# Pooled attention into a tanh-shrink MLP: group 0's second matmul, the x blocks of batch 1 and the loads around them in another order

## The chip, the cores and the metric

One NeuronCore of a Trainium2 chip. The metric is the device time of one launch in microseconds (us). The profile is one execution of the kernel, taken by the hardware profiler. Engines: PE (TensorE matmul; PEld is its weight load), DVE (VectorE), ACT (ScalarE), POOL (GpSimd) and SP (SyncE, which here only issues DMAs).

## The reference

`q`, `k`, `v` are (8, 8, 576, 64) float32: 8 batches, 8 heads, 576 rows, head width 64. `w_in` is 512 x 2048 and `w_out` 2048 x 512.

```
k_p = k.reshape(B, H, 72, 8, 64).mean(axis=3);  v_p likewise
scores = q @ k_p^T / 8;  attn = softmax(scores);  x = attn @ v_p
x = x.transpose(0, 2, 1, 3).reshape(4608, 512)
h = x @ w_in;  g = h - tanh(h);  out = g @ w_out       # out (4608, 512) float32
```

## The kernel before

**Work and tiling.** The 4608 rows are cut into nine groups of 512. Group g below 8 is the first 512 rows of batch g, and group 8 holds the last 64 rows of all eight batches. A group has two stages. The h stage computes 16 blocks of `h` (128 hidden columns by 512 rows, four matmuls each) with an ACT tanh and a DVE subtraction behind each, and leaves `Gt`. The output stage multiplies `Gt` by `w_out`. While group g is in its output stage, the attention of batch g+1 (scores, exp, product with v, normalising) is threaded between the matmuls, and the loads of batch g+2 run ahead of that.

**Order.** The schedule is written out by hand: each engine and each DMA queue executes its instructions in the order in which the Python code emits them, and semaphores are placed where one engine's data meets another's. So a move of a line in the code is a move in the in-order queue of every engine which that line uses.

**Group 0** is different from the others. Its output stage is direct: `mlp_o(0, tb, qd, gts)` (L611) is a unit of four 512-column matmuls, for row block `tb` (0 to 3) and a quarter `qd` of the hidden dimension. The quarters take `w2b` in the order of `W2_ORDER`, blocks 0, 8, 4, 12, which is the order in which the four parts of `w_out` arrive. Each row block has its PSUM bank (1, 2, 3, 0). With `qd == 3` the unit also copies the finished bank to `O`: on DVE for `tb` 0 and 1 (L626), on ACT for 2 and 3 (L628). The units double as filler between the steps of batch 1's attention (L1021 to L1085), which has to be done before group 1 can start:

- `k_transpose(1)`, `q_pe_transpose`, `q_pe_tail`, `scores_wide`, `scores_ends`: PE transposes and scores, evacuated by DVE and ACT.
- `pool_v1(0, 2)` and `pool_v1(2, 4)` (L300): DVE adds that pool `v_raw` and write `VB`, one half of the heads each. They wait for two POOL-queue loads of v.
- `av(1, blk, ...)` (L540): six matmuls `E` by `VB`, then on DVE a reciprocal (L522) and a multiplication (L523) into `x_sb`. `turn1(blk)` (L1000) transposes that block on PE (L566) and copies it on ACT into `xT[1]` (L573). Both take PSUM banks 4 to 7 in turn.
- `x_dma_transpose(1, 2)` and `k_dma_transpose(2)`: DMA transposes on SP's queue.
- `pool_k(2)`, `pool_v(2)`, `k_place(2)`: POOL work for batch 2, followed in group 1 by `v_spread(2)`, three small DMAs on POOL's queue that build `VB` for batch 2.

**Weight sums.** Groups 1 to 8 use a seven-product scheme for the output stage and need sums of quarters of `w_out`, kept in `w2s`. `sum0` to `sum3` (DVE, L673) build slots 0 to 3, in halves that start at hidden block 0 or 4; `negated` (ACT, L1004) builds slot 4; and `w_sum(b12, b22, b12, ALU.subtract)` replaces `b12` by `b22 - b12` in place, as one DVE instruction over all eight blocks. All must be emitted before group 1's products, and `b12` is also an input of `sum1`.

**Group 1's h stage** starts at L1087. `h_pair(1, p, b0, ...)` (L641) fills two PSUM banks, `b0` and `b0 + 1`, with b0 = 6, 4, 2, 6, 0, 2, 4 for p = 0 to 6; so p = 3 reuses the banks of p = 0, and p = 5 those of p = 2. ACT's tanh (L646) and DVE's subtraction (L647) read both banks; the bank pair is free when the subtraction is done. Between them ACT casts q of batch 2 for p = 2, 3, 4 (`q_cast_part`, L196 and L201) and SP issues its DMA transposes (L214, L219).

**Loads on SP's queue** around the change, in order: `load_k(2)` (held until the last v load of batch 1 has landed), `load_v(2)`, `load_q(2)`, the two transposes named above, `load_k(3)` (L1082), q's transposes of batch 2, both stores of group 0 (L1098, L1099), `load_v(3)`, `load_q(3)`. Later the transposes of batch 2's x (`x_dma_transpose`, L551) follow on the same queue, and group 2's first `h` matmuls wait for them.

**Start of the kernel.** The x of batch 0 is transposed on PE in four steps `x0_turn(blks, half, b0, eng)` (L939), through PSUM bank `b0` and an ACT copy into `xT[0]`; `h_part` (L958) computes the first blocks of `h` between them. `mlp_h(0, i, ...)` computes the later ones, in bank `i % 5`. `warm_pe` issues matmuls on zeros.

Of the kernel before, what the change touches and what calls it, by code (L numbers as in the profile page):

```python
# [12 lines left out]
ALU = mybir.AluOpType  # L13
# [14 lines left out]
TG = 512  # L28
# [15 lines left out]
def kernel(  # L44
# [9 lines left out]
    nc = tc.nc  # L54
# [9 lines left out]
    def bank(i, shape):  # L64
        n = 1
        for d in shape[1:]:
            n *= d
        v = PS[:, i, 0:n]
        if len(shape) == 3:
            return v.rearrange("p (a b) -> p a b", a=shape[1])  # L70
        if len(shape) == 4:
            return v.rearrange("p (a b c) -> p a b c", a=shape[1], b=shape[2])
        return v
# [226 lines left out]
    def pool_v1(ta, tb, eng=nc.vector):  # L300
        r = v_raw[1].rearrange("p t (j d) -> p t j d", d=D)
        for n in (4, 2, 1):
            eng.tensor_tensor(  # L303
                out=r[:, ta:tb, 0:n, :],
                in0=r[:, ta:tb, 0:n, :],
                in1=r[:, ta:tb, n : 2 * n, :],
                op=ALU.add,
            )
        if ta == NM:
            return v_left(VB[1], r[:, NM, 0:1, :], eng)  # L310
        return v_main(VB[1], r[:, ta:tb, 0:1, :], nc.vector, ta, tb)
# [228 lines left out]
    def av(b, blk, alloc, both):  # L540
        x_sb = x_block(b, blk)
        if both:
            av_both(b, blk, x_sb)
        else:
            for half in range(2):
                av_half(b, blk, half, x_sb, alloc)
        return x_sb
# [57 lines left out]
    def mlp_h(g, i, gts, pool):  # L605
        mlp_h_mms(g, i, 0, NFB, pool)
        mlp_h_act(i, gts)
# [3 lines left out]
    def mlp_o(g, tb, qd, gts):  # L611
        if qd == 0:
            o_tiles[tb] = bank((1, 2, 3, 0)[tb], [128, DM])
        o_ps = o_tiles[tb]
        i0 = W2_ORDER[qd]
        for i in range(i0, i0 + 4):
            nc.tensor.matmul(
                o_ps[:, :],
                lhsT=gts[i][:, tb * 128 : (tb + 1) * 128],
                rhs=w2b[:, i, :],  # L620
                start=(i == 0),
                stop=(i == NHID - 1),
            )
        if qd == 3:
            if tb < 2:
                nc.vector.tensor_copy(out=O[:, tb, :], in_=o_ps[:, :])  # L626
            else:
                nc.scalar.copy(out=O[:, tb, :], in_=o_ps[:, :])  # L628

    def h_mms(g, i, dst, t0=0, t1=4):  # L630
        x = xT[g % 2] if g < NB else xT_last
# [40 lines left out]
    def w_sum(out, a, b, op, eng=nc.vector, k0=0, k1=NP):  # L672
        return eng.tensor_tensor(  # L673
            out=out[:, k0:k1, :], in0=a[:, k0:k1, :], in1=b[:, k0:k1, :], op=op
        )
# [136 lines left out]
    for m, base, step, cm in (  # L812
# [6 lines left out]
            out=m,  # L819
            in_=m,  # L820
# [118 lines left out]
    def x0_turn(blks, half, b0, eng):  # L939
        n = len(blks)  # L940
        ps = bank(b0, [128, 2, n, 128])
        for i, blk in enumerate(blks):
            for f in range(2):
                nc.tensor.matmul(
                    ps[:, f, i, :],
                    lhsT=x0[:, blk, half, 2 * f : 2 * f + 2, :].rearrange("p h d -> p (h d)"),
                    rhs=ident[:, :],
                    start=True,
                    stop=True,
                )  # L950
        eng(
            out=xT[0][:, blks[0] : blks[0] + n, 2 * half : 2 * half + 2, :].rearrange(
                "p i f c -> p f i c"
            ),
            in_=ps,
        )
# [11 lines left out]
    x0_turn((0, 1), 0, 0, nc.scalar.copy)  # L968
    av_pair(1, 1, 1)
    warm_pe(1, b0=5)  # L970
    x0_turn((2, 3), 0, 0, nc.scalar.copy)
    for i, b0 in ((0, 6), (1, 7), (2, 5)):
        h_part(i, 0, 0, b0)
    x0_turn((0, 1), 1, 4, nc.scalar.copy)
    h_part(3, 0, 0, 3)
    for i in range(3):
        h_part(i, 0, 1)
    x0_turn((2, 3), 1, 0, nc.scalar.copy)
    nc.scalar.copy(out=q_bf[:QT, R, :, :], in_=t0[:QT, :, R, :])
    h_part(3, 0, 1)  # L980
    for i in range(4):
# [6 lines left out]
    mlp_h(0, 4, gts, bank(4, [128, TG]))  # L988

    for i in range(5, NHID):  # L990
        mlp_h(0, i, gts, bank(i % 5, [128, TG]))
        if i == 7:
            q_pe_tail(0)
        if i == 9:
            scores_tail(0)
        if i == 11:
            ps_a.n = 0
            av(0, 4, ps_any, True)
            x_dma_transpose(0, 2)
    def turn1(blk):  # L1000
        x_pe_transpose(1, blk, x_pairs[1, blk // 2][:, blk % 2])

    def negated(n):
        nc.scalar.mul(  # L1004
            out=w2s[:, 4, 4 * n : 4 * n + 4, :], in_=b22[:, 4 * n : 4 * n + 4, :], mul=-1.0
        )

    ps_a = Banks(4, 5, 6, 7)
    def sum0(k0):
        return w_sum(w2s[:, 0, :, :], b11, b22, ALU.add, k0=k0, k1=k0 + 4)  # L1010

    def sum1(k0):
        return w_sum(w2s[:, 1, :, :], b11, b12, ALU.add, k0=k0, k1=k0 + 4)

    def sum2(k0):
        return w_sum(w2s[:, 2, :, :], b21, b22, ALU.add, k0=k0, k1=k0 + 4)
# [13 lines left out]
    k_transpose(1, ps_any, (nc.vector.tensor_copy, nc.vector.tensor_copy))  # L1030
    q_pe_transpose(1, (0, 1), "act")
    mlp_o(0, 3, 0, gts)
    pool_v1(0, 2)
    q_pe_transpose(1, (2, 3), "act")
    q_pe_tail(1)
    scores_wide(1, (0,))
    sum1(0)
    mlp_o(0, 0, 1, gts)
    scores_wide(1, (1,))
    mlp_o(0, 1, 1, gts)  # L1040
    scores_wide(1, (2, 3))
    scores_ends(1)
    negated(0)
    sum2(0)
    sum0(0)
    sum3(0)
    pool_v1(2, 4)
    mlp_o(0, 2, 1, gts)
    mlp_o(0, 3, 1, gts)
    mlp_o(0, 0, 2, gts)  # L1050
    mlp_o(0, 1, 2, gts)
    ps_a.n = 0
    after(load_k(2), v1_last)
    load_v(2)
# [2 lines left out]
    av(1, 1, ps_any, True)  # L1057
    sum1(4)
    sum0(4)
    mlp_o(0, 2, 2, gts)  # L1060
    turn1(0)
    mlp_o(0, 3, 2, gts)
    turn1(1)
    av(1, 2, ps_any, True)
    av(1, 3, ps_any, True)
    negated(1)
    sum3(4)
    mlp_o(0, 0, 3, gts)
    turn1(2)
    mlp_o(0, 1, 3, gts)  # L1070
    turn1(3)
    av(1, 4, ps_any, True)
    x_pairs.pop((1, 0))
    x_pairs.pop((1, 1))
    x_dma_transpose(1, 2)
    pool_k(2, nc.gpsimd)
    k_dma_transpose(2)
    mlp_o(0, 2, 3, gts)
    mlp_o(0, 3, 3, gts)
    sum2(4)  # L1080
    w_sum(b12, b22, b12, ALU.subtract)
    load_k(3)  # L1082
    pool_v(2, nc.gpsimd, (0, 1))
    k_place(2, nc.gpsimd.tensor_copy)
    pool_v(2, nc.gpsimd, (2,))  # L1085
# [1 line left out]
    for g in range(1, NG):  # L1087
        nb = g + 1 if g + 1 < B else None
        nn = g + 2 if g + 2 < B else None
        for p in range(NP - 1):  # L1090
            if g == 1 and 2 <= p < 5:
                q_cast_part(2, p - 2)
                q_dma_transpose(2, p - 2)
            if nb is not None and g > 1 and p < 3:
                q_cast_part(nb, p)
            h_pair(g, p, ((6, 4, 2, 6, 0, 2, 4) if g == 1 else (0, 2, 4, 6, 0, 2, 4))[p], p % 2)
            if g == 1 and p == 4:
                store(0, 0, 2, nc.sync)  # L1098
                store(0, 2, 4, nc.sync)  # L1099
                load_v(3)  # L1100
                load_q(3)
                v_spread(2, nc.gpsimd)
            if 3 <= p < 6:
                sum_p(2 * p - 6, 2 * p - 4)
            if g > 1 and p == 0:
                if nb is not None:
                    k_dma_transpose(nb)
                store(g - 1, 2, 4, nc.gpsimd)
                store(g - 1, 0, 2, nc.gpsimd)
                if nb is not None:  # L1110
                    k_place(nb, nc.gpsimd.tensor_copy)
            if nb is not None and g > 1 and p < 3:
                q_dma_transpose(nb, p)
            if nb is not None and g > 1 and p == 2:
                v_spread(nb)
                if nn is not None:
                    load_k(nn)
                    load_v(nn)
                    load_q(nn)
        h_one(g, NP - 1, 1, 0, 2)  # L1120
        h_one(g, NP - 1, 0, 1, 3)
        sum_p(6, 8)
        sum_q(0, 4)
        sum_q(4, 8)
        if nb is not None:
            sum_d(0, 2)
            sum_d(2, 4)
        ps_a = Banks(2, 3, 4, 5, 0, 1)
        for u in range(14):
            n, half = u // 2, u % 2  # L1130
            bk, lhs, rhs = products[n]
            if n == 6 and g == NG - 1:
                break
            product(g, bk, lhs, rhs, 4 * half, 4 * half + 4, n < 2)
            if half:
                after_product(g, n)
            if nb is not None:
                if u == 0:
                    head_scores(nb, (0, 1))
                if u == 2:  # L1140
                    head_scores(nb, (2, 3), True)
                if u in (5, 6, 7, 8, 10):
                    blk = (5, 6, 7, 8, 10).index(u)
                    av(nb, blk, ps_b1, True)
                    if blk in (1, 3, 4):
                        x_dma_transpose(nb, blk // 2)
                if u == 6 and nn is not None:
                    pool_k(nn, nc.gpsimd)
                    pool_v(nn, nc.gpsimd)
        if g < NG - 1:  # L1150
            nc.scalar.copy(out=O[:, 0:2, 0:HD], in_=chain(g, C1))  # L1151
# [37 lines left out]
```

## Time and profile before

| what | value |
| --- | --- |
| median of 3 runs | 285.57 us (285.42 to 286.19) |
| the profiled execution | 285.73 us, span 283.9 us |
| granted TensorE clock | 1.00 |
| PE busy | 274.5 us, 97% of the span |
| DVE, ACT, POOL busy | 79%, 55%, 42% |
| HBM read, written | 36.70 MB, 9.44 MB |

The span runs from the first to the last instruction that the profile holds; 1.8 us of the profiled execution lie around it. A line of a timeline gives the start, the duration, engine, code line, operation, output and input tiles, shapes and a count; a bracket at its end is the idle time of the engine before it and what ended that. A duration counts waiting inside the engine too. Matmul durations include the pipeline's drain, so consecutive matmuls overlap: the distance between starts is their real cost.

Landmarks in the span: group 0's h stage ends and its output stage starts at 32.01 us; group 1's h stage starts at 52.96, its products at 67.52; group 2's h stage starts at 82.50. Each later group takes about 28.8 us up to the last ones.

### The profile page before, as it was taken

The page shows a single profiled execution, that of the slowest core. Times are in us where ns is not written, and L with a number is a line of the kernel's source. Part 1 is how long each engine was busy: PE and PEld are TensorE (multiplying, and loading weights), DVE is VectorE, ACT ScalarE, POOL GpSimd, SP SyncE. Part 2 cuts the span into 40 slices and gives each one's busy share as a digit, 9 for nine tenths or more (in the row PEclk, how much of TensorE's full clock was granted, in tenths as well). Part 3 has the DMA queues.
Part 4 walks back from the last instruction along what each step waited for, and adds up shares of the span by engine and source line. Part 5 has one row for each costly group of instructions (what it writes and reads, how often), then busy time and mean ns, then how long its engine had stood idle before and what let it go on. Part 6 is the DMA issues. An engine that isn't in the chain of part 4 may idle for free.

```text
span 283.9 us, 5492 instructions
## 1 busy us (share of the span) xinstructions
PE 274.5 (97%) x2174; PEld 180.9 (64%) x2174; DVE 224.2 (79%) x337; ACT 154.8 (55%) x207; POOL 118.5 (42%) x132
## 2 busy tenths in 40 slices
PE   7999998999999999999999999999999999999993
PEld 2574544645884589448944895489547954884583
DVE  5758968999966997599859985998599849936983
ACT  4757482487437662766285718670867056216610
POOL 8853601992497029801990199009900210010000
PEclk9999999999999999999999999999999999999999
DMA  6999999899968794789488948896640440011014
GB/s 247 236 212 277 225 243 279 240 216 270 275 98 198 245 311 89 172 257 328 85 134 300 333 85 136 250 331 133 125 151 1 77 157 2 0 72 79 0 39 111
DMA packets 66491, 49.82 MB, mean 175 GB/s; under 512 B 42104, under 2 KB 55944, under 8 KB 66466
## 3 DMA queue, kind: packets, MB, share of 16 engines
q1 hardware_dynamic: 55538, 33.87, 46.9%
q0 software_dynamic: 8736, 13.77, 19.8%
q10 hardware_dynamic: 2192, 1.84, 2.2%
q8 instruction: 17, 0.28, 0.4%
q14 instruction: 8, 0.07, 0.1%
HBM read 36.70 MB, written 9.44 MB: 163 GB/s over the span
## 4 chain that ended last, share of the span: by engine, by line
PE 75%; DMA 12%; DVE 9%; POOL 2%; issue 1%; SPq 0%; DVEq 0%
PE PS L633 37%; PE PS L690 33%; DMA v_raw<-in_v_dram 8%; PE PS L446 3%; PE PS L472 2%; DVE w2s L673 2%; DMA k_raw<-in_k_dram 2%; DMA xT<-x_sb 2%; DVE x_sb L523 2%; DVE v_raw L303 1%; DVE w2b L673 1%; DVE rden L522 0%; DVE O L626 0%; DVE Gt L647 0%; POOL w2s L841 0%
## 5 line engine op out<-in xcount | busy, mean ns | idle before, releaser
L633 PE MATMUL PS<-xT,w1b 128*128 128x512 bf16 (+1 forms) x504 | 98.3, 355 | 1.1 <-DVE Gt L647 0.6
L647 DVE TENSOR_TENSOR Gt<-PS,TS 128x1024 bf16<-128x1024 f32 x56 | 68.3, 1220 | 32.2 <-ACT TS L646 32.1
L633 PEld LDWEIGHTS <-w1b 128*128 128x128 f16 x576 | 56.3, 98 | 54.2 <-issue 1.5
L646 ACT ACTIVATE TS<-PS 128x1024 f32<-128x1024 f32 x56 | 57.4, 1024 | 30.8 <-PE PS L633 28.2
L734 POOL TENSOR_TENSOR m<-O,m 128x512 f32<-128x512 f32 x6 | 7.6, 1261 | 77.1 <-ACT m L732 63.7
L690 PE MATMUL PS<-w2s,Dg 128*128 128x256 f16 x256 | 30.2, 272 | 0.0
L467 ACT ACTIVATE E<-PS 72x1024 bf16<-72x1024 f32 (+1 forms) x30 | 26.1, 930 | 3.9 <-PE PS L446 3.7
L690 PEld LDWEIGHTS <-Gt 128*128 128x128 bf16 x256 | 23.5, 98 | 7.0 <-issue 2.5
L261 POOL TENSOR_TENSOR k_raw<-k_raw 128x512 f32<-128x512 f32 (+2 forms) x13 | 21.1, 1638 | 16.3 <-DMA k_raw<-in_k_dram 16.3
L690 PEld LDWEIGHTS <-P 128*128 128x128 bf16 x256 | 24.5, 98 | 3.0
L690 PEld LDWEIGHTS <-Dg 128*128 128x128 bf16 x256 | 24.6, 98 | 2.8
L655 DVE TENSOR_TENSOR P<-Gt 128x1024 bf16<-128x1024 bf16 x32 | 21.9, 686 | 0.5
L706 POOL DMA_DIRECT2D out_dram<-O x14 | 7.7, 554 | 31.6 <-DVE O L744 29.5
L741 ACT COPY m<-PS 128x512 f32<-128x512 f32 x8 | 4.7, 586 | 29.6 <-PE PS L690 29.6
L665 DVE TENSOR_TENSOR Dg<-Gt 128x1024 bf16<-128x1024 bf16 x32 | 20.4, 681 | 0.0
L523 DVE TENSOR_TENSOR x_sb<-PS,rden 128x512 bf16<-128x512 f32 x28 | 19.4, 691 | 1.0
L282 POOL TENSOR_TENSOR v_raw<-v_raw 128x512 f32<-128x512 f32 (+1 forms) x12 | 19.6, 1656 | 0.0
L690 PE MATMUL PS<-w2s,Gt 128*128 128x256 f16 x128 | 16.4, 273 | 0.0
L690 PE MATMUL PS<-w2b,P 128*128 128x256 f16 x128 | 16.3, 273 | 0.0
L690 PE MATMUL PS<-w2b,Gt 128*128 128x256 f16 x128 | 16.3, 272 | 0.0
L690 PE MATMUL PS<-w2s,Q 128*128 128x256 f16 x128 | 16.3, 272 | 0.0
L1151 ACT COPY O<-PS 128x512 f32<-128x512 f32 x7 | 4.1, 586 | 21.9 <-PE PS L690 21.9
(124 smaller groups left out, 400.4 us busy)
## 6 DMA issues: line engine op xcount, KB each, us to landing
k_raw<-in_k_dram SPq DMA_DIRECT2D x7, 1024.0 KB, 5.9
out_dram<-O POOLq DMA_DIRECT2D x14, 512.0 KB, 4.3
v_raw<-in_v_dram SPq DMA_DIRECT2D x6, 1024.0 KB, 8.1
q_raw<-in_q_dram SPq DMA_DIRECT2D x6, 1024.0 KB, 11.4
w1b<-in_moe_w_in_dram POOLq DMA_DIRECT2D x4, 512.0 KB, 13.3
w2b<-in_moe_w_out_dram POOLq DMA_DIRECT2D x4, 512.0 KB, 21.8
v_raw<-in_v_dram POOLq DMA_DIRECT2D x2, 512.0 KB, 21.2
out_dram<-O SPq DMA_DIRECT2D x2, 512.0 KB, 4.2
```

The lines of the kernel that those rows point to most:

```text
L261: eng.tensor_tensor(out=r[:, ta:tb, 0:4, :], in0=r[:, ta:tb, 0:4, :], in1=r[:, ta:tb, 4:8, :], op=ALU.add,)
L282: eng.tensor_tensor(out=r[:, ta:tb, 0:4, :], in0=r[:, ta:tb, 0:4, :], in1=r[:, ta:tb, 4:8, :], op=ALU.add,)
L446: nc.tensor.matmul(dst, lhsT=kv[a * D : (a + 1) * D, m, :], rhs=rhs, start=True, stop=True,)
L467: nc.scalar.activation(out=e, in_=ps, func=ACT.Exp, scale=SCALE)
L523: nc.vector.tensor_tensor(out=x_sb[:, :, :, :], in0=ps[:, :, :, 0:D], in1=rden[:, :, :, :].to_broadcast([128, 2, 4, D]), op=ALU.mult,)
L633: nc.tensor.matmul(dst[:, t0 * 128 : t1 * 128], lhsT=w1b[:, fb, i * 128 : (i + 1) * 128], rhs=x[:, t0:t1, fb, :], start=(fb == 0), stop=(f ...
L646: nc.scalar.activation(out=t2, in_=PS[:, b0 : b0 + 2, :], func=ACT.Tanh)
L647: nc.vector.tensor_sub(out=Gt[:, p, :, :], in0=PS[:, b0 : b0 + 2, :], in1=t2)
L655: nc.vector.tensor_tensor(out=P[:, a:b, :], in0=Gt[:, a:b, 0, :], in1=Gt[:, a:b, 1, :], op=ALU.add)
L665: return nc.vector.tensor_tensor(out=Dg[:, a:b, :, :], in0=Gt[:, a:b, :, 0:HT], in1=Gt[:, a:b, :, HT:TG], op=ALU.subtract,)
L673: return eng.tensor_tensor(out=out[:, k0:k1, :], in0=a[:, k0:k1, :], in1=b[:, k0:k1, :], op=op)
L690: nc.tensor.matmul(part(g, bk, tt), lhsT=lhs(k, slice(tt * 128, (tt + 1) * 128)), rhs=rhs[:, k, :], start=(first and k == 0 and (tt == 0 o ...
```

## The change

- `mlp_o` copies all four finished banks on ACT.
- In the start, two of the four `x0_turn` go through bank 5 instead of 0, the third block of `h` moves from bank 5 to 0, and block 5 of `h` from bank 0 to 5.
- `sum1(0)`, `sum2(0)`, `sum0(0)` are emitted ahead of `pool_v1(0, 2)`, instead of behind it; `sum3(0)` stays.
- The remaining units of group 0 come about one unit earlier against batch 1's steps: one more unit stands ahead of `av(1, 0)`, one now stands between `av(1, 2)` and `av(1, 3)`, and none of the last ones is left behind `k_dma_transpose(2)`. `negated(1)` moves ahead of `av(1, 2)`.
- The two stores of group 0 are issued on SP as soon as their units are emitted: the first ahead of `av(1, 3)`, the second behind `x_dma_transpose(1, 2)`; before, both stood in group 1 behind `h_pair` p = 4.
- `load_k(3)` moves from behind the weight sums into group 1 behind `h_pair` p = 4, directly ahead of `load_v(3)`; that is behind q's transposes of batch 2.
- The in-place `w_sum` is cut in two: blocks 0 to 3 where it was, blocks 4 to 7 behind `h_pair` p = 0 of group 1.

```diff
         if qd == 3:
-            if tb < 2:
-                nc.vector.tensor_copy(out=O[:, tb, :], in_=o_ps[:, :])
-            else:
-                nc.scalar.copy(out=O[:, tb, :], in_=o_ps[:, :])
+            nc.scalar.copy(out=O[:, tb, :], in_=o_ps[:, :])
...
     warm_pe(1, b0=5)
-    x0_turn((2, 3), 0, 0, nc.scalar.copy)
-    for i, b0 in ((0, 6), (1, 7), (2, 5)):
+    x0_turn((2, 3), 0, 5, nc.scalar.copy)
+    for i, b0 in ((0, 6), (1, 7), (2, 0)):
         h_part(i, 0, 0, b0)
...
-    x0_turn((2, 3), 1, 0, nc.scalar.copy)
+    x0_turn((2, 3), 1, 5, nc.scalar.copy)
...
-        mlp_h(0, i, gts, bank(i % 5, [128, TG]))
+        mlp_h(0, i, gts, bank(i % 5 if i > 5 else 5, [128, TG]))
...
     mlp_o(0, 3, 0, gts)
+    sum1(0)
+    sum2(0)
+    sum0(0)
     pool_v1(0, 2)
     q_pe_transpose(1, (2, 3), "act")
     q_pe_tail(1)
     scores_wide(1, (0,))
-    sum1(0)
     mlp_o(0, 0, 1, gts)
     scores_wide(1, (1,))
     mlp_o(0, 1, 1, gts)
     scores_wide(1, (2, 3))
     scores_ends(1)
     negated(0)
-    sum2(0)
-    sum0(0)
     sum3(0)
     pool_v1(2, 4)
     mlp_o(0, 2, 1, gts)
     mlp_o(0, 3, 1, gts)
     mlp_o(0, 0, 2, gts)
     mlp_o(0, 1, 2, gts)
+    mlp_o(0, 2, 2, gts)
     ps_a.n = 0
     after(load_k(2), v1_last)
     load_v(2)
...
     sum1(4)
     sum0(4)
-    mlp_o(0, 2, 2, gts)
+    mlp_o(0, 3, 2, gts)
     turn1(0)
-    mlp_o(0, 3, 2, gts)
+    mlp_o(0, 0, 3, gts)
     turn1(1)
+    negated(1)
     av(1, 2, ps_any, True)
+    mlp_o(0, 1, 3, gts)
+    store(0, 0, 2, nc.sync)
     av(1, 3, ps_any, True)
-    negated(1)
     sum3(4)
-    mlp_o(0, 0, 3, gts)
     turn1(2)
-    mlp_o(0, 1, 3, gts)
+    mlp_o(0, 2, 3, gts)
     turn1(3)
     av(1, 4, ps_any, True)
     x_pairs.pop((1, 0))
     x_pairs.pop((1, 1))
     x_dma_transpose(1, 2)
+    mlp_o(0, 3, 3, gts)
+    store(0, 2, 4, nc.sync)
     pool_k(2, nc.gpsimd)
     k_dma_transpose(2)
-    mlp_o(0, 2, 3, gts)
-    mlp_o(0, 3, 3, gts)
     sum2(4)
-    w_sum(b12, b22, b12, ALU.subtract)
-    load_k(3)
+    w_sum(b12, b22, b12, ALU.subtract, k1=4)
...
             h_pair(g, p, ((6, 4, 2, 6, 0, 2, 4) if g == 1 else (0, 2, 4, 6, 0, 2, 4))[p], p % 2)
+            if g == 1 and p == 0:
+                w_sum(b12, b22, b12, ALU.subtract, k0=4)
             if g == 1 and p == 4:
-                store(0, 0, 2, nc.sync)
-                store(0, 2, 4, nc.sync)
+                load_k(3)
                 load_v(3)
                 load_q(3)
                 v_spread(2, nc.gpsimd)
```

## The prediction, made before the run

> **What bounds the kernel now.** I read the page, then the list of waits of PE, then the timelines of all engines from 32 to 84 us, and the DMA issues. The page first:
>
> ```profile
> PE 274.5 (97%) x2174; PEld 180.9 (64%) x2174; DVE 224.2 (79%) x337; ACT 154.8 (55%) x207; POOL 118.5 (42%) x132
> ```
>
> PE has 9.4 us of idle time in 283.9. From group 2 on, the chain of waits runs through PE alone to the last copy, so whatever PE saves before 84 us should arrive at the end. The waits of PE:
>
> ```profile
> PE PS L487 <- DVE VB L323: 1.1, 1, 1.1
> PE PS L633 <- DVE Gt L647: 0.6, 1, 0.6
> PE PS L633 <- DMA xT<-x_sb: 0.5, 1, 0.5
> ...
> PE PS L487 <- ACT xT L573: 0.2, 1, 0.2
> ```
>
> All four lie between 43 and 84 us. The first three in PE's timeline, with the matmuls ahead of two of them:
>
> ```profile
> 43.51 0.34 PE L487 MATMUL PS<-VB,E 128*128 128x130 bf16 x3
> 44.95 0.68 PE L487 MATMUL PS<-VB,E 128*128 128x130 bf16 x9 [1.10 <-DVE VB L323]
> ...
> 58.89 8.79 PE L633 MATMUL PS<-xT,w1b 128*128 128x512 bf16 x40 [0.57 <-DVE Gt L647]
> ...
> 82.50 1.04 PE L633 MATMUL PS<-xT,w1b 128*128 128x256 bf16 x8
> 84.03 13.12 PE L633 MATMUL PS<-xT,w1b 128*128 128x256 bf16 x64 [0.49 <-DMA xT<-x_sb]
> ```
>
> Costs by distance of starts in that timeline: an mlp_o unit 0.87 (46.62 to 47.48), an av 0.35 (50.88 to 51.23), a turn 0.24 (46.38 to 46.62). So the waits really cost more than the brackets say: 44.95 - (43.51 + 3 x 0.058) = **1.27**; at 48.54 (waiting for ACT's copy of xT) 48.54 - (47.70 + 9 x 0.058) = **0.32**; at 58.89, where p 0 to 2 need 1.74 + 2 x 1.73, 58.89 - 58.16 = **0.73**; at 84.03, 84.03 - (82.50 + 8 x 0.1085) = **0.66**.
>
> Behind the second stands DVE, held up by POOL:
>
> ```profile
> 53.88 1.61 DVE L673 TENSOR_TENSOR w2s<-w2b 128x1024 f16<-128x1024 f16 x1
> 55.42 2.29 DVE L673 TENSOR_TENSOR w2b<-w2b 128x2048 f16<-128x2048 f16 x1
> 57.62 3.59 DVE L647 TENSOR_TENSOR Gt<-PS,TS 128x1024 bf16<-128x1024 f32 x3
> ...
> 51.45 1.88 POOL L267 TENSOR_TENSOR k_raw<-k_raw 128x640 f32<-128x640 f32 x1
> 53.41 1.53 POOL L270 TENSOR_TENSOR kd<-k_raw 128x640 bf16<-128x640 f32 x1
> 54.90 4.47 POOL L282 TENSOR_TENSOR v_raw<-v_raw 128x512 f32<-128x512 f32 x2
> ```
>
> The same sum of 1024 columns takes 0.6 while POOL is idle (four in 2.40 at 40.65 in the chain). Here it ends 0.55 after POOL's L270 (54.94, 55.49), the next POOL instruction ends 1.13 after that (56.62), the 2048-column sum 1.09 after that (57.71): the two engines take turns.
>
> **What the Trainium skill says.** "SBUF — State Buffer", section "Who interferes with whom": a DVE instruction with two SBUF inputs and a GpSimd instruction that reads SBUF exclude each other, each for its whole length. The trace agrees to the 0.01 us just given. "DMA: Bandwidth & Descriptors", section "Queues, rings and completion order": descriptors of one queue are consumed in ring order, and a DMA engine takes turns between queues. The trace agrees with the first: q of batch 3, issued at 68.49, lands after 10.8 us at 79.3, and both x transposes issued behind it (76.87, 79.13) take 4.9 us instead of 3.1 in the next group. Turn-taking between queues is not shown cleanly.
>
> **Part by part.**
>
> *Banks of x0_turn.* The second turn waits for ACT's copy out of bank 0 (15.89 + 0.59 = 16.48; it starts at 16.53), where PE would be free at 16.26: 0.2 us. But PE then waits at the k transposes for kd, which DVE ends at 34.50 behind a DMA (PE: 34.60), and at the first unit of quarter 1 (37.11) for w2b, issued at 12.99 and landing 24.1 later, 37.09. Worth **0.0**; were that load sooner, -0.2.
>
> *Three sums ahead of pool_v1(0, 2).* DVE idles 2.61 us (36.09 to 38.70) for v. sum1 fits at once, sum2 and sum0 need the weights of 37.09: done by 38.3, still ahead of v. Behind VB's first half (40.65) only sum3 remains, to 41.3, and the second half of v lands at 22.7 + 19.6 = 42.3. pool_v1(2, 4) takes 1.86 (43.05 to 44.91), so VB is ready at 44.2 instead of 44.9. One more unit in front puts av(1, 0) at 43.51 + 0.87 = 44.38, its second half at 44.55. **The 1.27 go**, with 0.3 to spare.
>
> *Units between the steps.* PE now runs av 0 and 1 to 45.08, a unit to 45.95, turn 0 at 45.97 (x_sb: second half 44.55 + 0.44 + 0.24 + 0.69 = 45.92), a unit, turn 1, av 2 to 47.66, a unit to 48.53, av 3 (ACT's turn 1 copy is done at 48.3: **the 0.32 go**), turn 2, a unit to 49.98, turn 3 at 50.11 (DVE's x_sb at 50.07, a new wait of 0.13), av 4, a unit: group 1 starts at **51.57 instead of 52.96**. ACT carries two more copies (2 x 0.59, from DVE's 2 x 0.67) and negated's 1.06 sooner; its queue (0.5 a copy) ends turn 3's copy at 51.2 and the last copy of O at 52.2, ahead of PE's need (51.57 for bank 6 and the first two blocks, 52.0 for bank 7) and of the first tanh (53.6). Nothing queued there delays PE.
>
> *DVE up to Gt of p 0.* sum3(4) still waits for POOL and ends at 51.92; POOL's k load (48.3) hasn't moved. The two O copies (1.27) are gone, so av 4's multiplication ends at 52.8, and sum2 takes its turn at POOL's next end: 53.33 to 53.88. L270 then to 55.28, the half w_sum to 55.83, Gt of p 0 to 56.98 (1.15 as before). PE wants p 3 at 51.57 + 5.20 = 56.77, and gets it at 57.02 instead of 58.89: **gain 1.87 up to here**, the wait being 0.25 now.
>
> *The second half of w_sum* then asks for the port at about 56.9; POOL's L282 ends 55.83 + 1.13 = 56.96. **The order is not shown by any row.** If DVE gets it, w_sum costs 0.55 and Gt of p 2 ends at about 59.9, ahead of PE's p 5 (57.02 + 3.46 = 60.48): nothing lost. If POOL gets it, w_sum waits for L282's second half (1.66): Gt p 1 60.4, Gt p 2 61.6, and p 5 waits 1.16. I take the first, since DVE's next instruction shows up 0.09 before its predecessor's end, POOL's only 0.04.
>
> *Stores.* Two of 0.5 MB, issued at 49.8 and 54.0 on SP instead of 65. In ring order they stand behind q of batch 2 (lands 44.84 + 11.4 = 56.2) and fill a gap: 84 to 116 GB/s from 54 to 58. Cost on q **0**; without ring order, up to 1.05 MB at 340 GB/s (319 to 353 in the stretches from 44 to 54), 3.1 us. On SP, the first store waits for ACT's second copy and nothing is ready behind it before x_end at 52.8; the second is reached at 54.0, after its copy (52.2) and before kd (55.3), so neither holds up a transpose's issue. They delay the k transpose behind them to about 61.5, which POOL wants at 60.8 (k_place), so v_spread moves 0.7 later.
>
> *load_k(3)* leaves the place ahead of q's transposes, which then land by about 65; needed at 66.6. It starts at 62 with v and q behind. Group 2's row of loads took 14.0 from the first issue (93.50) to q's landing (96.03 + 11.5 = 107.5), so q lands at 76 to 77 instead of 79.3. x's second transpose, issued 1.87 sooner at 77.26, lands at 80.4 to 81.7; PE needs it at 82.50 - 1.87 + 0.87 = 81.5. **0.5 of the 0.66 go.** POOL wants k at 74.5; it lands at about 68.
>
> *Sum* on the profiled execution: 285.73 - 1.87 - 0.5 = 283.4; this execution lies 0.16 over the median, so **283.2**.
>
> **Rivals.**
>
> 1. *POOL gets the port first*: 1.87 - 1.16 + 0.5 = 1.2 gained, **284.3**. For it: the two requests lie within 0.1 us.
> 2. *The stores share bandwidth with q of batch 2.* q 3.1 late gives tanh of p 2 at 61.3, Gt at 62.6, p 5 waits 2.1: 285.57 - 1.87 + 2.1 - 0.5, about **285.3**. Against it: the ring order seen with the x transposes.
> 3. *v_spread becomes the bound; slower.* Its three small DMAs go over POOL's queue, at 64 to 65.5. Before, only stores and the start of v's load were near, and the last landed after 2.6 us (67.4). Now 3.4 MB on SP's queue are under way until about 76.5. av of batch 2 needs VB at 74.21 - 1.87 = 72.3. If the small packets are held back until the loads drain, av waits 4.2: 285.57 - 1.87 + 4.2, **287.9** with the x wait kept. It decides the sign from a landing at about 74.2 on. Against it: turn-taking, as the skill states, would cost only some 3 us.
> 4. *The order changes but the landings rule*: v's second half or kd land as much later as PE comes sooner; **285.5**. Against it: those loads don't depend on PE.
>
> **Numbers.** Forecast 0.47 (own range 282.7 to 283.8), rival 1 0.27 (283.9 to 284.7), rival 2 0.10, rival 3 0.09, rival 4 0.07. A difference of 0.3%, 0.86 us, is about what a measurement of this kernel can tell from no change. Faster (below 284.7): 0.47 + 0.26 + 0.01 = 0.74; slower (above 286.4): 0.09 and 0.02 of rival 2's upper end, 0.11; the rest 0.15. Range 282.6 to 285.4: it leaves out rival 3, part of rivals 2 and 4, and the tail below.
>
> **What would show it.** The VB wait and the ACT xT wait gone from PE's waits, group 1's first h matmul at 51.6, p 3 at 57.0, two DVE w2b sums with the second at 57 (or at 58.7: rival 1, with a wait of PE at L633 near 60.5), q's casts no later than 56.3 (else rival 2), the xT wait at most 0.2. Wrong would be a wait of PE at L472 on VB (rival 3), or group 1 starting as late as before.

## The result, and the profile after

| kernel | median us (range, runs) | ratio to before (95% interval) |
| --- | --- | --- |
| before | 285.57 (285.02 to 286.19, 7) | |
| changed | 284.43 (283.54 to 284.93, 7) | 0.9957 (0.9938 to 0.9977) |

The change saves 0.43%, 1.14 us (the interval is 0.66 to 1.77 us), where 2.37 were forecast (285.57 - 283.2). Executions more than 1.5% slower than the fastest of the same kernel are left out of all medians and ratios, here and below. The profiled execution of the changed kernel took 284.74 us with a span of 282.9. In its code the lines behind `mlp_o` stand three lower: L633 is L630, L647 L644, L673 L670, L690 L687.

Its waits of PE, in the columns total, times, longest:

```profile
PE PS L352 <- DVE kd L270: 1.4, 1, 1.4
...
PE PS L630 <- DMA xT<-x_sb: 0.5, 1, 0.5
```

Three of the four waits of before are gone: L487 for VB, L487 for xT, L633 for Gt. The xT wait of 0.5 stayed. New at the top is L352, the transposes of k ahead of batch 1's scores, which wait for `kd`. PE's timeline from there to group 2:

```profile
31.48 2.75 PE L617 MATMUL PS<-w2b,Gt 128*128 128x512 f16 x12
35.65 0.45 PE L352 MATMUL PS<-ident,kd 128*128 128x128 bf16 x5 [1.41 <-DVE kd L270]
...
45.48 0.86 PE L487 MATMUL PS<-VB,E 128*128 128x130 bf16 x12
...
52.67 14.00 PE L630 MATMUL PS<-xT,w1b 128*128 128x256 bf16 x72
66.50 1.04 PE L687 MATMUL PS<-w2s,Gt 128*128 128x256 f16 x8
...
81.57 1.04 PE L630 MATMUL PS<-xT,w1b 128*128 128x256 bf16 x8
83.09 3.19 PE L630 MATMUL PS<-xT,w1b 128*128 128x256 bf16 x18 [0.48 <-DMA xT<-x_sb]
```

The line at 45.48 holds both halves of two av without a stop between them; before, the second half stood still for VB. The line at 52.67 is the h stage of group 1 without a stop, up to its products. The same points of both profiles, side by side:

| point of PE | before | changed | gain so far |
| --- | --- | --- | --- |
| group 0's output stage starts | 32.01 | 31.48 | 0.53 |
| transposes of k (L352) | 34.60 | 35.65 | -1.05 |
| group 1's h stage starts | 52.96 | 52.67 | 0.29 |
| its products start | 67.52 | 66.50 | 1.02 |
| group 2's h stage starts | 82.50 | 81.57 | 0.93 |
| the matmul behind the xT wait | 84.03 | 83.09 | 0.94 |
| end of the span | 283.9 | 282.9 | 1.0 |

From L352 to group 1 the changed kernel takes 17.02 instead of 18.36: **1.34 gained**, where the prediction had 52.96 - 51.57 = 1.39. From group 1's start to its products it takes 13.83 instead of 14.56: **0.73 gained**, the p 3 wait. But PE was already 1.05 behind the old kernel when that stretch began, since `kd` was late, and nothing came at xT.

DVE's timeline answers the question who gets the port that DVE and POOL share:

```profile
54.38 2.03 DVE L670 TENSOR_TENSOR w2b<-w2b 128x1024 f16<-128x1024 f16 x1
56.34 1.21 DVE L644 TENSOR_TENSOR Gt<-PS,TS 128x1024 bf16<-128x1024 f32 x1
57.47 0.68 DVE L670 TENSOR_TENSOR w2b<-w2b 128x1024 f16<-128x1024 f16 x1
```

The second half of `w_sum` took 0.68: DVE had the port at once, at 57.47. POOL's second L282 starts at 57.52 and has to wait for it, 2.32 where it took 1.66 before:

```profile
57.52 2.32 POOL L282 TENSOR_TENSOR v_raw<-v_raw 128x768 f32<-128x768 f32 x1
```

There is no wait of PE at L472 on VB, so rival 3 didn't come. Two questions were left: why is `kd` late in this kernel, and where did the half microsecond of xT go? My theory then was that the changed kernel is worth some 2 us, and that a late k hides 1.05 of it.

### The profile page after: what moved, and what is told of

The parts are those of the page before. It is cut to its first block, busy times and chain, and to the rows that moved or that the text cites. A ratio compares the mean times of both kernels' runs of the same rounds, so it can differ in the third digit from the quotient of the medians.

```text
span 282.9 us, 5497 instructions
## 1 busy us (share of the span) xinstructions
PE 274.3 (97%) x2174; PEld 180.8 (64%) x2174; DVE 222.6 (79%) x336; ACT 155.2 (55%) x209; POOL 118.5 (42%) x132
## 4 chain that ended last, share of the span: by engine, by line
PE 83%; DMA 10%; POOL 3%; DVE 1%; issue 1%; SPq 0%; POOLq 0%; DVEq 0%
PE PS L630 39%; PE PS L687 33%; DMA w1b<-in_moe_w_in_dram 5%; PE PS L617 4%; DMA k_raw<-in_k_dram 3%; PE PS L446 3%; PE PS L472 2%; DMA xT<-x_sb 2%; POOL k_raw L261 1%; DVE x_sb L523 1%; PE PS L487 1%; POOL v_raw L827 1%; POOL k_raw L267 1%; PE PS L398 1%; PE PS L566 0%
## 5 line engine op out<-in xcount | busy, mean ns | idle before, releaser
L630 PE MATMUL PS<-xT,w1b 128*128 128x512 bf16 (+1 forms) x504 | 98.1, 355 | 0.5 <-DMA xT<-x_sb 0.5
L644 DVE TENSOR_TENSOR Gt<-PS,TS 128x1024 bf16<-128x1024 f32 x56 | 68.3, 1220 | 32.1 <-ACT TS L643 32.1
L630 PEld LDWEIGHTS <-w1b 128*128 128x128 f16 x576 | 56.4, 98 | 53.5 <-issue 0.7
L643 ACT ACTIVATE TS<-PS 128x1024 f32<-128x1024 f32 x56 | 57.3, 1024 | 30.3 <-PE PS L630 28.2
L687 PE MATMUL PS<-w2s,Dg 128*128 128x256 f16 x256 | 30.2, 272 | 0.0
L687 PEld LDWEIGHTS <-Gt 128*128 128x128 bf16 x256 | 23.6, 98 | 6.8 <-issue 2.3
L687 PEld LDWEIGHTS <-P 128*128 128x128 bf16 x256 | 24.5, 98 | 3.0
L687 PEld LDWEIGHTS <-Dg 128*128 128x128 bf16 x256 | 24.6, 98 | 2.8
L282 POOL TENSOR_TENSOR v_raw<-v_raw 128x512 f32<-128x512 f32 (+1 forms) x12 | 19.2, 1616 | 0.0
L687 PE MATMUL PS<-w2s,Gt 128*128 128x256 f16 x128 | 16.4, 273 | 0.0
L687 PE MATMUL PS<-w2b,P 128*128 128x256 f16 x128 | 16.3, 273 | 0.0
L687 PE MATMUL PS<-w2b,Gt 128*128 128x256 f16 x128 | 16.3, 272 | 0.0
L687 PE MATMUL PS<-w2s,Q 128*128 128x256 f16 x128 | 16.3, 272 | 0.0
## 6 DMA issues: line engine op xcount, KB each, us to landing
w1b<-in_moe_w_in_dram POOLq DMA_DIRECT2D x4, 512.0 KB, 13.9
```

The source lines that it names most:

```text
L282: eng.tensor_tensor(out=r[:, ta:tb, 0:4, :], in0=r[:, ta:tb, 0:4, :], in1=r[:, ta:tb, 4:8, :], op=ALU.add,)
L630: nc.tensor.matmul(dst[:, t0 * 128 : t1 * 128], lhsT=w1b[:, fb, i * 128 : (i + 1) * 128], rhs=x[:, t0:t1, fb, :], start=(fb == 0), stop=(f ...
L643: nc.scalar.activation(out=t2, in_=PS[:, b0 : b0 + 2, :], func=ACT.Tanh)
L644: nc.vector.tensor_sub(out=Gt[:, p, :, :], in0=PS[:, b0 : b0 + 2, :], in1=t2)
L687: nc.tensor.matmul(part(g, bk, tt), lhsT=lhs(k, slice(tt * 128, (tt + 1) * 128)), rhs=rhs[:, k, :], start=(first and k == 0 and (tt == 0 o ...
```

## The experiments

All kernels were timed in turns with the kernel before on the same chip: 285.48 in one series of turns, 285.42 in two others (medians of 38 to 43 runs); the ratio is not the quotient of two medians. Three measures are read from the one profile of each: *start* is group 1's first h matmul and *q* the landing of q of batch 2, both counted from SP's issue of `load_k(2)`, so that what shifts everything ahead of it drops out (that load waits for the last v of batch 1, so a v that lands later doesn't show in *start*); *half* is PE's return to L687 behind the scores of batch 2, counted from the span's start (69.04 before, 68.10 in the changed kernel).

| kernel | median | ratio (95% interval) | start | q | half |
| --- | --- | --- | --- | --- | --- |
| before, first profile | 285.57 | | 10.62 | 13.9 | 69.04 |
| before again | 285.65 | 1.0012 (0.9999 to 1.0025) | 10.61 | 14.0 | 68.85 |
| before, start banks | 285.70 | 1.0005 (0.9990 to 1.0021) | 10.62 | 13.9 | 68.56 |
| before, copies on ACT | 285.11 | 0.9995 (0.9978 to 1.0011) | 10.61 | 14.2 | 68.36 |
| changed, copies on DVE | 285.15 | 0.9996 (0.9983 to 1.0008) | 10.69 | 14.1 | 68.64 |
| changed, first profile | 284.43 | 0.9957 (0.9938 to 0.9977) | 9.64 | 14.0 | 68.10 |
| changed again | 284.35 | 0.9966 (0.9950 to 0.9983) | 9.25 | 15.3 | 68.56 |
| changed, q of batch 3 on POOL | 284.17 | 0.9967 (0.9946 to 0.9987) | 9.85 | 14.0 | 67.43 |
| changed, k of batch 3 as before | 284.83 | 0.9985 (0.9962 to 1.0009) | 9.46 | 14.9 | 68.41 |
| changed, w_sum in one | 284.61 | 0.9977 (0.9955 to 1.0000) | 9.39 | 15.0 | 68.10 |
| changed, stores as before | 286.47 | 1.0037 (1.0019 to 1.0054) | 9.43 | 14.4 | 68.65 |
| changed, casts later, q on POOL | 284.14 | 0.9953 (0.9941 to 0.9965) | 9.23 | 14.5 | 67.51 |
| changed, first store later | 283.94 | 0.9962 (0.9944 to 0.9980) | 9.49 | 13.8 | 67.23 |
| the same, q on POOL | 284.36 | 0.9962 (0.9948 to 0.9976) | 9.75 | 14.1 | 68.14 |

In thirteen of these fourteen profiled executions the time is 216.1 to 216.9 us more than *half* (284.74 - 68.10 = 216.6 in the changed kernel's first). Only with the stores as before is it 217.9, and there the xT waits are the longest. So what the kernels differ by is settled by then, save for the xT wait.

### Is the late k part of the change?

**The changed kernel again**, nothing edited.

> The changed kernel once more. Theory (landings): the time above 283.4 us is PE waiting for the k of batch 1 (kd) and for the second part of w_out, whose landing differs by about 1 us between executions; so the times lie between 283.4 and 285, and the profiled one is 283.4 plus its wait of PE at the k transposes (bracket, 0 to 1.4 us), give or take 0.4. Rival (the change itself makes these loads later): the wait at the k transposes is 1.2 to 1.6 us again, whatever the time of the execution.

The late k does not come in every execution of the changed kernel. Here the load is issued at 18.95 instead of 20.24, and group 1 starts at 51.69. But the time is no better, 285.21 for this execution. Its PE timeline shows why:

```profile
51.69 8.82 PE L630 MATMUL PS<-xT,w1b 128*128 128x256 bf16 x48
61.03 5.48 PE L630 MATMUL PS<-xT,w1b 128*128 128x512 bf16 x24 [0.52 <-DVE Gt L644]
...
68.22 0.41 PE L446 MATMUL PS<-qT,KB 64*72 64x512 bf16 x2 [0.50 <-DVE Gt L644]
```

The wait at 61.03 is that of p 5 for Gt of p 2. Behind it stands ACT, which waits for q of batch 2 before a cast and comes late to the tanh of p 2:

```profile
57.75 1.04 ACT L196 CAST q_bf<-q_raw 128x1024 bf16<-128x1024 f32 x1 [1.31 <-DMA q_raw<-in_q_dram]
58.71 1.02 ACT L643 ACTIVATE TS<-PS 128x1024 f32<-128x1024 f32 x1
```

The idea that the time is a constant plus the wait for `kd` falls: k was issued 1.29 sooner and group 1 started 0.98 sooner than in the first profile, and behind q of batch 2 PE was 0.46 later (*half*). That is rival 2's chain, at a smaller price.

**The kernel before again.**

> The kernel before once more, for a second profile. Theory (in the kernel before, the wait for VB takes up what the landings of k and of w_out's second part differ by): group 1's h stage starts at 43.5 + 9.5 us behind the same landings of v, that is 10.6 to 10.8 us after load_k(2) is issued (52.96 - 42.34), whatever PE waits for kd and w2b; q of batch 2 lands 13.9 us after load_k(2); times 285.0 to 286.5. Rival: the start of group 1 moves with kd's landing one to one, and the wait for VB stays at 1.1 us.

Start is 10.61 again, though PE waits 0.7 for `kd` ahead of it; the wait for VB is still there, 0.09 shorter:

```profile
45.41 0.68 PE L487 MATMUL PS<-VB,E 128*128 128x130 bf16 x9 [1.01 <-DVE VB L323]
```

In the kernel before, PE is released by VB, which hangs on v and DVE, so a `kd` that is late by less than the VB wait is hidden under it; in the changed kernel it isn't. (v itself landed 0.46 later here, and group 1 started 0.45 later in the span.) A k as late as that of the changed kernel's first profile came in none of the four profiles of the old order. This execution also has no wait at p 3: k of batch 2 landed later, POOL came later to the port and DVE's sum got in front. So the 0.73 of the first profile are not in every execution, and were not the change's to save each time.

### What each part is worth

**Start banks alone**, on the kernel before.

```diff
-    x0_turn((2, 3), 0, 0, nc.scalar.copy)
+    x0_turn((2, 3), 0, 5, nc.scalar.copy)
...
-    x0_turn((2, 3), 1, 0, nc.scalar.copy)
+    x0_turn((2, 3), 1, 5, nc.scalar.copy)
```

> The kernel before with only the banks of the start changed (the second x0_turn, the third and sixth block of h). Theory: group 0's output stage starts 0.2 us earlier, and the waits for kd, w2b and VB take all of it; time within 0.15 us of the kernel before. Rival: the 0.2 us pass on to the end.

Start 10.62, as before: nothing gained, as forecast.

**Copies on ACT alone**, on the kernel before; and **the changed kernel with two copies on DVE**.

```diff
-            nc.scalar.copy(out=O[:, tb, :], in_=o_ps[:, :])
+            if tb < 2:
+                nc.vector.tensor_copy(out=O[:, tb, :], in_=o_ps[:, :])
+            else:
+                nc.scalar.copy(out=O[:, tb, :], in_=o_ps[:, :])
```

> The kernel before with all four copies of O on ACT and nothing else of the change. Theory (the copies only make room on DVE behind av 4; the wait for VB is another matter): the wait for VB stays at 1.0 to 1.1 us, group 1's h stage starts 10.5 to 10.7 us after load_k(2) as before, no wait for Gt at p 3; the x and q landings bound what follows, time 0 to 0.3 us below the kernel before. Rival (DVE's copies are what the gain is made of): time 0.7 us or more below.

> The copies of O's first two row blocks on DVE again, all else as changed. Theory (freeing DVE of 1.3 us, and of one turn at the port behind it, is what took away the wait of 0.73 us at h_pair p 3): Gt of p 0 ends 1 us or more later than in the changed kernel with the same landing of k, PE waits 0.5 to 1.3 us for Gt at p 3; time 0.5 to 1.0 us above the changed kernel. Rival (the cut of the weight sum or the earlier sums did it): no wait at p 3, time within 0.3 us.

Alone, the copies gain nothing at start (10.61). Without them, the rest of the change shows no gain either: start is 10.69, the time that of the kernel before (0.9996, 0.9983 to 1.0008). PE's waits have a new entry, turns 2 and 3 waiting for DVE's x_sb:

```profile
PE PS L566 <- DVE x_sb L523: 0.6, 2, 0.4
```

That start is partly a late `kd`, for which PE waits 1.1 in this profile. The stretch from av 0 to group 1 lies behind that wait:

```profile
45.01 0.86 PE L487 MATMUL PS<-VB,E 128*128 128x130 bf16 x12
...
52.98 0.49 PE L633 MATMUL PS<-xT,w1b 128*128 128x256 bf16 x3
```

It took 7.97 here, and 7.19 or 7.20 in all nine profiles of the new order with the copies on ACT. The old order took 9.33 to 9.45, with the copies on ACT too (9.43); one unit of 0.87 in it now stands ahead of av 0, which leaves 8.46 to 8.58. So of some 1.3 gained in this stretch 0.8 need the copies on ACT, and the copies need the new order to be worth anything. Which of the new order's own parts, the earlier sums or the moved units, does the rest was not tested. The place that had been expected, p 3, was wrong: there was no wait there. In that profile POOL got the port first, though, which is rival 1's order (PE had no wait from it at p 5, since group 1 started only at 52.98):

```profile
57.18 2.23 DVE L673 TENSOR_TENSOR w2b<-w2b 128x1024 f16<-128x1024 f16 x1
```

```profile
57.05 1.81 POOL L282 TENSOR_TENSOR v_raw<-v_raw 128x768 f32<-128x768 f32 x1
```

POOL asked 0.13 ahead of DVE; in the changed kernel DVE was 0.05 ahead. "SBUF — State Buffer", section "Who interferes with whom", of the Trainium skill has whoever issues first hold the pair for its whole instruction; both profiles agree. The margin is small but it is no throw of a coin: in all eight profiles of the new order with the copies on ACT and the sum in two, DVE's record starts 0.03 to 0.05 ahead and its sum takes 0.68.

**w_sum in one piece**, in the changed kernel.

```diff
-    w_sum(b12, b22, b12, ALU.subtract, k1=4)
+    w_sum(b12, b22, b12, ALU.subtract)
...
-            if g == 1 and p == 0:
-                w_sum(b12, b22, b12, ALU.subtract, k0=4)
```

> The in-place weight sum in one piece again, all else as changed. Theory (DVE and POOL take turns at the port, and Gt of p 0 is what p 3 waits for): Gt of p 0 ends 0.55 us or more later, PE waits 0.5 to 0.8 us at h_pair p 3 (bracket; none in the changed kernel), time 0.5 to 0.8 us above the changed kernel, about 285.0. Rival (the earlier start of DVE's queue is enough): no wait at p 3 and the time within 0.2 us.

PE's list of waits has no entry at p 3 here either. By the distance of starts, 57.11 - (51.66 + 5.20), it lost 0.25 there; in the changed kernel's two profiles it lost nothing. The uncut sum took 2.56, and Gt of p 0 and 1 came out behind it:

```profile
53.37 2.56 DVE L670 TENSOR_TENSOR w2b<-w2b 128x2048 f16<-128x2048 f16 x1
55.85 2.34 DVE L644 TENSOR_TENSOR Gt<-PS,TS 128x1024 bf16<-128x1024 f32 x2
```

So the cut is worth 0.25 at p 3 in this profile. Whether it buys time isn't resolved: 284.61 against 284.35 for the changed kernel in the same turns, with intervals that overlap widely.

**Stores as before**, in the changed kernel: both behind p 4, ahead of `load_k(3)`.

```diff
     mlp_o(0, 1, 3, gts)
-    store(0, 0, 2, nc.sync)
...
     mlp_o(0, 3, 3, gts)
-    store(0, 2, 4, nc.sync)
...
             if g == 1 and p == 4:
+                store(0, 0, 2, nc.sync)
+                store(0, 2, 4, nc.sync)
                 load_k(3)
```

> Both stores of group 0 back behind h_pair p = 4 of group 1, ahead of load_k(3); all else as changed. Theory (the earlier stores share the DMA engines with q of batch 2): q lands 13.8 to 14.1 us after the issue of load_k(2), as in the kernel before, instead of 15.0 to 15.3 in three of the five profiles of changed kernels; ACT's first cast of q waits at most 0.3 us for it, and PE has no wait for Gt at h_pair p 5 or at the scores (L446); the xT wait stays at 0.5 us or grows by up to 0.5, since the stores now stand ahead of k, v and q of batch 3; time 0 to 0.5 us below the changed kernel. Rival (q's landing scatters whatever the stores do): q lands 15 us after load_k(2) here too, or the time is that of the changed kernel within 0.2 us.

The only kernel slower than before, by 0.37% (0.19 to 0.54), and 2.0 us above the changed one (286.47 and 284.43, in different turns). Both x transposes of batch 2 are late:

```profile
82.48 1.05 PE L630 MATMUL PS<-xT,w1b 128*128 128x256 bf16 x8 [0.19 <-DMA xT<-x_sb]
84.86 5.35 PE L630 MATMUL PS<-xT,w1b 128*128 128x256 bf16 x28 [1.34 <-DMA xT<-x_sb]
```

SP's timeline of that kernel has 1 MB of stores and 3.4 MB of loads in one row, and q, issued last at 67.95, lands 13.1 later, at 81.05:

```profile
62.74 1.04 SPq L703 DMA_DIRECT2D out_dram<-O  x2
63.83 0.78 SPq L150 DMA_DIRECT2D k_raw<-in_k_dram  x1
...
67.95 0.60 SPq L184 DMA_DIRECT2D q_raw<-in_q_dram  x1
...
76.48 4.70 SPq L551 DMA_TRANSPOSE xT<-x_sb  x2
```

In the changed kernel q lands at 78.8, before at 79.3. So k moved behind q's transposes *needs* the stores in front. What the early stores would be worth with k in its old place wasn't run.

**k of batch 3 as before**, in the changed kernel.

```diff
     w_sum(b12, b22, b12, ALU.subtract, k1=4)
+    load_k(3)
...
             if g == 1 and p == 4:
-                load_k(3)
```

> load_k(3) back at its old place behind the first weight sum, all else as changed. Theory: the move of load_k(3) gained nothing, since it pushed 1.1 MB in front of q of batch 3; with k back, q lands about 2.5 us sooner (76 instead of 78.8), the xT wait of 0.48 us goes, and q's own transposes still land before the scores need them; time 0.3 to 0.7 us below the changed kernel. Rival (as predicted: the move shortens the xT wait): the wait grows to 0.7 us or more, or PE waits for qT at the scores (66.6 us), and the time is 0.2 us or more above the changed kernel.

q of batch 3 landed at 76.7 and the xT wait fell to 0.15, but q's transposes of batch 2 were issued over 6.0 us instead of 3.1, and PE waited 0.3 at p 3, 0.5 at L446. The median is 0.5 above the changed kernel's in the same turns; the intervals overlap. The move does no harm; that it helps isn't shown.

**q of batch 3 on POOL's queue**, in the changed kernel, so that the x transposes have SP's queue to themselves.

```diff
-                load_q(3)
                 v_spread(2, nc.gpsimd)
+                load_q(3, eng=nc.gpsimd)
```

> q of batch 3 is loaded on the POOL queue behind v_spread, not on SP's queue. Theory (ring order: the x transposes of batch 2 stand behind q of batch 3 in SP's queue): the x transposes land in 3.0 to 3.5 us instead of 4.8, PE's wait of 0.48 us for xT is gone, and the time is 0.5 to 0.7 us below the changed kernel, about 283.8. Rival (the DMA engines' bandwidth is short, on whatever queue): the wait stays at 0.4 us or more and the time within 0.2 us of the changed kernel.

The xT wait falls to 0.17, though the second transpose still takes 4.5 us. The median moves by 0.2 against the changed kernel, which isn't resolved.

### Does the store delay q of batch 2?

In seven profiles with the first store at about 50 us, q came 14.0 to 14.1 after `load_k(2)` in the three in which that store was issued 7.9 to 8.4 after it, and 14.5 to 15.3 in the four with 7.5 to 7.7. In the four profiles of the old order, with no store there, it came after 13.9 to 14.2, and with the stores as before after 14.4. So 14.5 may be scatter, 14.9 to 15.3 hardly. In these profiles a PE that is earlier issues the store earlier, and gets q later.

The DMA packets of the traces, sorted by size (q's load has 1024 of 1 KB, the two stores have 256 of 4 KB), show how the two meet. In all seven profiles the store's first packet starts 3.5 to 4.4 after its issue, so the store does stand behind most of q. But 71 to 163 of q's packets start after that first packet in the four profiles with q at 14.5 to 15.3, and 25 to 47 in the other three. Store and load run beside each other at q's end. Whether the store holds q up there, or a q that lags leaves more packets for that end, the packets don't tell. Two kernels were made to test it.

**First store with the second**, at 54 instead of 50.

```diff
     mlp_o(0, 1, 3, gts)
-    store(0, 0, 2, nc.sync)
...
     mlp_o(0, 3, 3, gts)
+    store(0, 0, 2, nc.sync)
     store(0, 2, 4, nc.sync)
```

> The first store of group 0 is issued together with the second, behind x_dma_transpose(1, 2) at about 54 us, instead of at 50; all else as changed. Theory (in the changed kernels whose first store was issued within 7.75 us of load_k(2), q of batch 2 landed 14.5 to 15.3 us after it, in those with 7.85 us or more 14.0): q lands 14.0 us after load_k(2) (13.8 to 14.2), ACT's first cast of q waits 0.4 us at most, no wait of PE at h_pair p 5; second half of the first product at most 25.3 us after load_k(2) (the changed kernel's two profiles: 25.1 and 26.1); time 0.2 to 0.5 us below the changed kernel's 284.4. Rival (q's landing scatters by itself): q lands 14.5 us or later here too, or the time is within 0.2 us of the changed kernel.

q after 13.8, at 56.15, and the cast comes without a wait:

```profile
56.44 1.04 ACT L196 CAST q_bf<-q_raw 128x1024 bf16<-128x1024 f32 x1
```

The DMA traffic of three stretches shows the store itself (last two columns: share of the DMA engines, GB/s). First the changed kernel again, then this one:

```profile
54.00:55.00 1.00, 1.00 (x7) 0.44 (x5) 1.00 (x1) 0.72 (x1) 1.00 (x1) 1.00 1.22 291
55.00:56.00 1.00, 1.00 (x6) 0.44 (x5) 1.00 (x2) 0.58 (x1) 1.00 (x2) 1.00 1.44 366
56.00:57.00 1.00, 1.00 (x6) 0.49 (x5) 1.00 (x2) 0.44 (x1) 1.00 (x2) 1.00 2.86 195
```

```profile
54.00:55.00 1.00, 1.00 (x6) 0.47 (x5) 1.00 (x1) 0.83 (x1) 1.00 (x2) 1.00 1.06 179
55.00:56.00 1.00, 1.00 (x7) 0.47 (x5) 1.00 (x2) 0.48 (x1) 1.00 (x1) 1.00 0.40 86
56.00:57.00 1.00, 1.00 (x7) 0.41 (x6) 1.00 (x2) 1.00 (x2) 1.00 (x2) 1.00 1.03 270
```

With the store in the queue the gap that the prediction wanted to fill is full, and q is not yet in. With the store at 54 none of q's packets starts after the store's first. 0.5 MB at the 335 GB/s of the stretch from 50 to 52 are 1.6 us; q was up to 1.3 late. q came on time in both kernels with the store at 54, this one and the next, with one profile of each. So the cause is well supported but not proven.

**The same with q of batch 3 on POOL's queue.**

> Both stores at 54 us and q of batch 3 on the POOL queue; all else as changed. Theory: q of batch 2 lands 14.0 us after load_k(2), the second half of the first product starts at most 25.3 us after it, and the xT wait is 0.2 us or less; time 0.4 to 0.9 us below the changed kernel, about 283.8. Rival: one wait is traded for another, time within 0.3 us of the changed kernel.

q after 14.1, the xT wait at 0.24; but `load_k` of batch 1 was issued at 20.27 here and PE waited 1.5 for `kd`. Over the kernel with the store alone no gain shows.

**q's casts, transposes and the loads behind them one h_pair later**, with q of batch 3 on POOL's queue.

```diff
-            if g == 1 and 2 <= p < 5:
-                q_cast_part(2, p - 2)
-                q_dma_transpose(2, p - 2)
+            if g == 1 and 3 <= p < 6:
+                q_cast_part(2, p - 3)
+                q_dma_transpose(2, p - 3)
...
-            if g == 1 and p == 4:
+            if g == 1 and p == 5:
```

> ACT's three casts of q of batch 2, with their transposes and the loads behind them, come one h_pair later, and q of batch 3 is loaded on the POOL queue; all else as changed. Theory (an early PE is held up by q of batch 2, which lands at a time that PE doesn't set, in front of the tanh of p 2): ACT no longer waits for q ahead of a tanh, PE has no wait for Gt at p 5 or at L446 even if q lands 15 us after load_k(2), and the xT wait is at most 0.3 us; what is left are the waits for kd and w2b near 34 to 38 us; time 0.5 to 1.0 us below the changed kernel, 283.4 to 283.9. Rival (the ACT and DVE queues are too full in group 1 whatever the order): waits for Gt of 0.5 us or more remain, time within 0.3 us of the changed kernel. Second rival: q's transposes land too late for the scores, a new wait at L446 on qT.

q after 14.5 costs nothing here, since the cast is no longer ahead of p 2's tanh: half is at 67.51. But all loads of batch 3 move back, v lands at 79.2, and the xT wait grows to 0.92. The ratio, 0.9953 (0.9941 to 0.9965), is level with the changed kernel's.

The lowest median is that of the later first store, 283.94, 1.5 under before (0.9962, 0.9944 to 0.9980). It is 0.4 to 0.5 under the changed kernel, and their intervals overlap, so it is a candidate and no proven improvement.

## Why the prediction was right, and what was mis-sized

The measured 284.43 lies in the prediction's range, but above the forecast's own 282.7 to 283.8, and the forecast gain of 2.37 lies outside the interval of the measured one. It lies where rival 1 was put (284.3; its sum gives 284.4), and rival 1 didn't come: DVE had the port first. So the number fell into a part of the range that was meant for another cause, which is luck. The two waits went as argued; half of the forecast gain was lost to terms that the sum put too high or at nothing.

**VB and ACT's xT, right.** Both waits went, and the stretch behind them gained 1.34. The prediction's own sum from av 0 to group 1, 51.57 - 44.38, is 7.19, and that is what nine profiles show. The measure *start* falls from 10.61 and 10.62 in four profiles of the old order to 9.23 to 9.85 in nine of the new: 0.8 to 1.4, 1.1 in the mean. In the span group 1 starts 0.9 sooner in the mean (52.94 and 52.05). Start banks 0.0, right. The port at the second half of `w_sum`, right in eight profiles of eight, by 0.03 to 0.05 us.

**p 3, right in mechanism, too large.** The forecast counted 1.87 up to p 3: 1.39 from the earlier start of group 1 and 0.48 from a shorter wait for Gt. The wait went, and all of 0.73 came in the first profile. But the time lost there is 0.73 in the first profile of before, 0.6 in that with the start banks, and next to nothing in before again (0.05) or with the copies on ACT. A duration out of one profile was taken for that of all.

**"Cost on q 0", mis-sized.** The step leaned on ring order: a store that is issued after q stands behind it. "DMA: Bandwidth & Descriptors", section "Queues, rings and completion order", says that order for each DMA engine by itself, and that completion does not follow the order of issue; the prediction took it for an order of whole transfers. The x transposes, which it read as agreement, are no good sign of it: the second still took 4.5 us with q on another queue. In the runs q landed up to 1.3 later with a store issued 5.0 to 5.2 us behind it, and on time with that store at 54. The term is 0 to 1.3, not 0. It takes back what an early PE gained: from group 1's start to *half* PE took 15.43 or 15.44 in the four profiles of the new order with the copies on ACT and q at 13.8 to 14.1, and 16.44 to 16.87 in the three with q at 14.9 to 15.3 (in two of these 0.25 and 0.45 of it were lost at p 3).

**Stores elsewhere, mis-sized the other way.** The step asked only what the stores cost at 50 and 54, not what they would cost if they stayed. Issued at 63, ahead of k, v and q of batch 3, they cost 2.0 us (284.43 to 286.47, in different turns), and the sum has no term for that: the early stores are what makes the move of k bearable.

**xT 0.5, mis-sized.** q of batch 3 was to land at 76 to 77, from the 14.0 us of group 2's row of loads; the row took 15.9 here (62.87 to 78.8), and the wait stayed. The second transpose took 4.8 us, where 3.1 to 4.4 were counted, and 4.5 even where q had left SP's queue or had landed at 76.7. What slows it isn't settled.

**Loads of the start, missing in the sum.** k of batch 1 was issued between 18.91 and 20.27 in the profiles. SP holds that load until a part of `w_in` has landed, and no line of the change moves that. It was late (20.24 and 20.27) in two profiles of ten that have the new order and in none of four that haven't, which is too few to tell the change from scatter. The prediction's av 0 at 44.38 came at 44.46 to 45.50. Before, the VB wait covered a `kd` late by less than it; with that wait gone, a late k reaches the end. Rival 4 said that the landings would take the gain: for part of it they do.

Summed: 0.8 to 1.4 at *start*, a late k already counted in it, 0 to 0.7 at p 3, nothing from xT, less up to 1.4 for a late q. The 1.14 measured lie in that; how the terms fall in each of the unprofiled runs isn't known.

## What to carry to other kernels

When a wait goes, list what it was covering: late loads in front of it were free while it stood, and enter the time once it is gone. Count a moved DMA against every transfer that is still under way on its queue, the earlier ones too, and ask also what it would cost to leave it in its place once its neighbours have moved. A wait of half a microsecond that hangs on when loads land should enter the sum with a range that starts at zero, since one profile shows one throw of the landings.

## What the runs showed of the hardware

- A load of 1 MB with a store of 0.5 MB issued 5.0 to 5.2 us behind it on the same queue landed 0.9 to 1.3 us late in three profiles of seven. The store's first packets started while 71 to 117 of the load's 1024 were still to start.
- The port that DVE and POOL share went to the engine whose record starts first, by margins of 0.03 to 0.05 us (DVE, eight profiles) and 0.13 us (POOL, one), worth 1.55 us in one sum (0.68 against 2.23).
- The second DMA transpose of x took 4.5 us with q's load on another queue, so q ahead of it on its own queue is not all that slows it.
- The same load at the start, k of batch 1, was issued up to 1.4 us apart in executions of like programs.
